# Attention into a Strassen-style MLP on one core: a new start-up order, other buffer counts, a new order at the end, and the sums of w_out moved from VectorE to GpSimd

## The chip, the core and the metric

The kernel runs on one core of a Trainium2 chip. The metric is the device time of one execution in microseconds (us), as the median over several executions. The profile of one execution gives a span that is 1.7 to 1.9 us shorter than its time (1.9 to 3.7 us in the three kernels below that begin with 92 short matmuls); spans are used only to say where time lies. A run that is over 1.5% above the fastest of the same kernel is called slow and set aside: medians are of the fast runs, and all profiles shown are of fast runs.

Names: PE is TensorE's matmuls, PEld its weight loads, DVE is VectorE, ACT is ScalarE, POOL is GpSimd. "L276" is line 276 of the kernel that the profile belongs to. The change shifts lines by five, so L672 before is L677 after (h in parts), L798 is L803 (products with w_out), L708 is L713 (h with whole 128x128 matmuls), L497 is L502 (scores), L509 is L514 (products with v), L619 is L624 (the multiplication of the silu).

## The reference

```python
# q, k, v: (8, 12, 448, 64)
scores = 1/sqrt(64) * (q @ k.T) - log(448)
attn   = 1 / (1 + exp(-scores))           # a sigmoid, no softmax
x      = (attn @ v) -> (3584, 768)
h      = x @ w_in                          # w_in  (768, 2048)
g      = h * sigmoid(h)
out    = g @ w_out                         # w_out (2048, 768), float32 out
```

## The kernel before

The kernel is a planner in Python. It keeps a model of each engine's time, decides from it in which order the instructions are emitted, and the result is one fixed stream for each engine. Twenty-four visits (four heads of one batch each) give scores, sigmoids and products with v; a piece of h takes all visits of its batch; fourteen row groups multiply g by w_out with seven products instead of eight. The seven products need sums of blocks of w_out, made once, and sums of blocks of g, made for each row group:

```python
    def tt(key, dur, deps, o, a, b_, op, prio=0):
        pl.op("DVE", dur, key, deps, lambda: nc.vector.tensor_tensor(o, a, b_, op), prio=prio)

    def sums_wo(f0, f1):                      # called for (0, 4) and (4, 8): eight sums of 128x1536
        ...
        tt(kk + (0,), d, dep, t1, a12, a11, sub, 5)
        tt(kk + (1,), d, [kk + (0,)], t2, a22, t1, sub, 5)
        tt(kk + (2,), d, [kk + (1,)], a12, a22, a12, sub, 5)
        tt(kk + (3,), d, [kk + (2,)], t4, a21, t2, sub, 5)
    ...
        def sums(self):                       # in each of 14 row groups: four sums of 128x1024
            ...
            tt(kk + (1,), 600, self.deps + old(0), s1, a21, a22, add, -1)
            tt(kk + (2,), 600, [kk + (1,)] + old(1), s2, s1, a11, sub, -1)
            tt(kk + (3,), 600, [kk + (2,), kk + (1,)], a21, a11, a21, sub, -1)
            tt(kk + (4,), 600, [kk + (2,)] + old(2), s4, a12, s2, sub, -1)
```

Both kinds of sum read two tiles in SBUF and write one there. That is the fact that this study turns on. The sums of g stand on VectorE in front of the silu multiplications, which empty the PSUM banks that TensorE needs for its next pieces of h.

Two other parts are used in the experiments. The buffer counts are `NTR = 4; NX = 4; NA = 10; NV = 6` (transposed k and q, loaded k and q, score tiles, v). And at the very start TensorE multiplies zeros to warm up, in 28 matmuls of 64x64 by 512 columns, before the first loads arrive:

```python
    def zeros(i, m):
        ...
                    nc.tensor.matmul(
                        pt[h][64 * j : 64 * j + 64, :], zero[64 * h : 64 * h + 64, :D], zero[64 * h : 64 * h + 64, :],
                        start=True, stop=True, skip_group_check=True,
                    )
```

## Time and profile before

| | before |
|---|---|
| time, median of 3 (lowest to highest) | 386.08 us (385.11 to 390.47) |
| span of the profiled execution, mean granted clock | 382.5 us, 0.996 |
| TensorE busy | 96% |
| first product with w_out starts | 86.66 us |
| one sum of g (128x1024) / of w_out (128x1536) on VectorE | 0.69 us / 0.95 us |

The prediction below shows the page's first lines, the stretches and the timelines. Two more things are needed for the comparison. First, on the page, the granted clock in 40 slices (tenths of full speed) and the chain of work that ended last, by engine and by line:

```profile
PEclk9999999999999999999999999999999999999998
...
PE 87%; DMA 7%; DVE 2%; POOL 1%; issue 1%; ACT 1%; DVEq 0%; POOLq 0%
```

The clock never falls, and TensorE carries 87% of the chain. Second, in the groups by shape, the first of the four sums of g, with its 14 executions, total busy us and mean ns; then two of these sums in VectorE's timeline, and the first product with w_out in TensorE's:

```profile
L276 DVE TENSOR_TENSOR gs<-gt 128x1024 f16<-128x1024 f16 x14 | 9.2, 688 | 0.2
...
80.04 0.68 DVE L276 TENSOR_TENSOR gs<-gt 128x1024 f16<-128x1024 f16 x1
...
81.10 0.69 DVE L276 TENSOR_TENSOR gs<-gs,gt 128x1024 f16<-128x1024 f16 x1
...
86.66 0.35 PE L798 MATMUL ps<-wo,gt 64*64 64x384 f16 x2
```

### The profile page before, as it was taken

The numbers are of one execution on the slowest core, as the hardware profiler recorded it, in microseconds if no ns is written. First come the engines' busy times: TensorE is split into PE (matmuls) and PEld (weight loads), VectorE is DVE, ScalarE is ACT, GpSimd is POOL, SyncE is SP. The second block draws the span as 40 slices with busy tenths as digits, with TensorE's granted clock in tenths as the row PEclk, the third lists the DMA queues.
The fourth block names the chain that finished last, engine by engine and source line by source line (L and its number), as shares of the span: only waits on it lengthen the run. The fifth ranks groups of instructions, "written<-read, shape, count | busy, mean of one in ns | idle before, by whom it ended". The sixth has DMA issues, their size and how long they took to land.

```text
span 382.5 us, 18036 instructions
## 1 busy us (share of the span) xinstructions
PE 367.3 (96%) x8028; PEld 305.3 (80%) x8028; DVE 203.6 (53%) x378; ACT 233.6 (61%) x506; POOL 65.0 (17%) x97
## 2 busy tenths in 40 slices
PE   6797998999999999999999999999999999999995
PEld 3565866787888989878998989878888898989763
DVE  3634988683454535454654556454645456455632
ACT  3975787677758866757637787686656863243110
POOL 9655413231220220220210220000000000000000
PEclk9999999999999999999999999999999999999998
DMA  7999999999999976993779998725132002400333
GB/s 102 196 209 205 208 209 203 157 160 152 176 194 207 135 112 130 180 189 71 96 115 181 154 143 116 124 49 79 43 71 60 3 2 47 105 22 5 74 90 90
DMA packets 80638, 46.52 MB, mean 122 GB/s; under 512 B 50609, under 2 KB 79793, under 8 KB 80561
## 3 DMA queue, kind: packets, MB, share of 16 engines
q0 software_dynamic: 25008, 22.81, 39.5%
q1 hardware_dynamic: 55552, 22.56, 35.8%
q8 instruction: 63, 1.03, 1.1%
q14 instruction: 15, 0.11, 0.1%
HBM read 45.61 MB, written 11.01 MB: 148 GB/s over the span
## 4 chain that ended last, share of the span: by engine, by line
PE 87%; DMA 7%; DVE 2%; POOL 1%; issue 1%; ACT 1%; DVEq 0%; POOLq 0%
PE ps L798 34%; PE ps L672 30%; PE ps L708 8%; PE ps L497 8%; PE ps L509 7%; DMA wi<-in_moe_w_in_dram 5%; DMA v<-in_v_dram 2%; DVE so L276 1%; PE ps L455 1%; POOL xk L219 1%; POOL xq L228 1%; DVE gt L619 0%; ACT at L947 0%; DVE xt L969 0%; DVE qT L469 0%
## 5 line engine op out<-in xcount | busy, mean ns | idle before, releaser
L672 PE MATMUL ps<-xt,wi 64*64 64x448 f16 x2304 | 164.1, 349 | 0.0
L540 ACT ACTIVATE at<-ps 128x448 f16<-128x448 f32 x252 | 121.9, 549 | 42.8 <-PE ps L497 38.7
L672 PEld LDWEIGHTS <-wi 64*64 64x64 f16 x2304 | 110.3, 107 | 14.5 <-issue 0.3
L619 DVE TENSOR_TENSOR gt<-ps,sg 128x448 f16<-128x448 f32 (+2 forms) x128 | 78.4, 622 | 78.9 <-ACT sg L614 78.6
L798 PE MATMUL ps<-wo,gt 64*64 64x384 f16 x1344 | 108.5, 323 | 0.0
L798 PEld LDWEIGHTS <-gt 64*64 64x64 f16 x1792 | 95.6, 107 | 11.7 <-issue 2.3
L614 ACT ACTIVATE sg<-ps 128x448 f16<-128x448 f32 (+2 forms) x128 | 70.2, 552 | 46.2 <-PE ps L672 31.2
L798 PE MATMUL ps<-so,gs 64*64 64x384 f16 x896 | 86.2, 323 | 0.2 <-issue 0.2
L798 PEld LDWEIGHTS <-gs 64*64 64x64 f16 x1344 | 76.2, 107 | 9.4 <-issue 1.1
L497 PE MATMUL ps<-qT,kT 64*64 64x448 f16 (+2 forms) x840 | 75.8, 316 | 2.1 <-DVE qT L469 0.8
L812 DVE SCALAR_TENSOR_TENSOR us<-ps,us 128x384 f32<-128x384 f32 x70 | 38.8, 555 | 48.7 <-PE ps L798 40.1
L947 ACT ACTIVATE at<-ps 128x512 f16<-128x512 f32 (+3 forms) x96 | 40.1, 520 | 15.6 <-PE ps L497 15.3
L708 PE MATMUL ps<-xt,wi 128*128 128x256 f16 (+1 forms) x384 | 43.3, 260 | 4.1 <-DMA wi<-in_moe_w_in_dram 2.7
L798 PE MATMUL ps<-so,gt 64*64 64x384 f16 x448 | 44.9, 323 | 0.5 <-issue 0.5
L798 PE MATMUL ps<-wo,gs 64*64 64x384 f16 x448 | 45.1, 323 | 0.0
L497 PEld LDWEIGHTS <-kT 64*64 64x64 f16 x840 | 33.8, 106 | 12.1 <-issue 7.5
L708 PEld LDWEIGHTS <-wi 128*128 128x128 f16 x384 | 32.3, 98 | 10.8 <-issue 6.7
L239 POOL DMA_DIRECT2D v<-in_v_dram x24 | 17.4, 724 | 138.7 <-PE ps L509 47.9
L509 PE MATMUL ps<-at,v 64*64 64x448 f16 (+2 forms) x840 | 40.2, 313 | 0.0
L819 ACT ACTIVATE us<-ps 128x384 f32<-128x384 f32 x28 | 14.0, 499 | 33.3 <-PE ps L798 32.7
L509 PEld LDWEIGHTS <-v 64*64 64x64 f16 x840 | 29.6, 107 | 5.2 <-issue 1.9
L552 DVE TENSOR_SCALAR xt<-ps 128x448 f16<-128x448 f32 x36 | 20.8, 620 | 21.0 <-PE ps L509 20.8
(33 smaller groups left out, 148.4 us busy)
## 6 DMA issues: line engine op xcount, KB each, us to landing
out_dram<-us SPq DMA_DIRECT2D x112, 96.0 KB, 2.7
xk<-in_k_dram POOLq DMA_DIRECT2D x24, 224.0 KB, 6.9
v<-in_v_dram POOLq DMA_DIRECT2D x24, 224.0 KB, 6.2
xq<-in_q_dram POOLq DMA_DIRECT2D x21, 224.0 KB, 8.5
wo<-in_moe_w_out_dram POOLq DMA_DIRECT2D x4, 768.0 KB, 15.4
wi<-in_moe_w_in_dram POOLq DMA_DIRECT2D x8, 192.0 KB, 7.2
wi<-in_moe_w_in_dram POOLq DMA_DIRECT2D x4, 384.0 KB, 9.7
qT<-xq SPq DMA_TRANSPOSE x32, 4.5
```

What stands on the lines that cost most here:

```text
L239: lambda: nc.gpsimd.dma_start(v16[n % NV], src(v, b, g)),
L497: nc.tensor.matmul(pt[r][64 * h : 64 * h + 64, lo : lo + (c1 - c0) * D], kT[n % NTR][64 * r : 64 * r + 64, i, 64 * h : 64 * h + 64], qT[n ...
L509: nc.tensor.matmul(pt[h][64 * j : 64 * j + 64, :N], v16[n % NV][64 * h : 64 * h + 64, j, c * D : (c + 1) * D], at[64 * h : 64 * h + 64, sl ...
L540: lambda r=r: nc.scalar.activation(at[:, sl, r], pt[r][:, :S], AF.Sigmoid, bias=NEG_LOG_S, scale=QKSCALE),
L552: lambda h=h: nc.vector.tensor_scalar_mul(x[:, 2 * g + h, :], pt[h][:, :S], SX), prio=-2,
L614: lambda: nc.scalar.activation(t[:, :ncol], src_, AF.Sigmoid, scale=ISX), prio=0,
L619: lambda: nc.vector.tensor_tensor(o, src_.rearrange("p (a t) -> p a t", a=nb), t[:, :ncol].rearrange("p (a t) -> p a t", a=nb), ALU.mult),
L672: nc.tensor.matmul(bank[64 * j : 64 * j + 64, z * N : z * N + N], wi[64 * h : 64 * h + 64, cc, f0 + 64 * j : f0 + 64 * j + 64], x[64 * h : ...
L708: nc.tensor.matmul(bank[:, z * N : z * N + N], wi[:, cc, fc * P : (fc + 1) * P], x[:, cc, self.c0 : self.c1], start=(cc == 0 and z == 0), ...
L798: nc.tensor.matmul(bank[64 * j : 64 * j + 64, :HE], lhs[64 * h : 64 * h + 64, c, 64 * j : 64 * j + 64], rhs[64 * h : 64 * h + 64, c, :], s ...
L812: lambda: nc.vector.scalar_tensor_tensor(o, bank[:, :HE], ISX, u, ALU.mult, ALU.add), prio=-2,
L947: lambda r=r, src_=src_: nc.scalar.activation(at[:, base : base + m, r, :N], src_, AF.Sigmoid, bias=NEG_LOG_S, scale=QKSCALE),
```

## The change

The intent: let readiness decide the order of the start-up instead of a fixed list; take 7.6 us of sums away from VectorE, which is busy there, and give them to GpSimd, which only issues loads; move buffers from v, k and q to score tiles; and interleave the last two row groups so that TensorE's matmuls keep overlapping. The core of the diff (the planner's loop for the middle is cut; it looks nine products ahead instead of six):

```diff
-    NTR = 4
-    NX = 4
-    NA = 10
-    NV = 6
+    NTR = 3
+    NX = 3
+    NA = 12
+    NV = 3
...
+    def tt_pool(key, n, deps, o, a, b_, op, prio=0):
+        pl.op("POOL", 100 + 2.2 * n, key, deps, lambda: nc.gpsimd.tensor_tensor(o, a, b_, op), prio=prio)
...
-        tt(kk + (0,), d, dep, t1, a12, a11, sub, 5)
-        tt(kk + (1,), d, [kk + (0,)], t2, a22, t1, sub, 5)
-        tt(kk + (2,), d, [kk + (1,)], a12, a22, a12, sub, 5)
-        tt(kk + (3,), d, [kk + (2,)], t4, a21, t2, sub, 5)
+        for z, (o, x_, y_) in enumerate(((t1, a12, a11), (t2, a22, t1), (a12, a22, a12), (t4, a21, t2))):
+            dz = dep if z == 0 else [kk + (z - 1,)]
+            if z in (0,1,2,3):
+                tt_pool(kk + (z,), (f1 - f0) * HE, dz, o, x_, y_, sub, 5)
...
-                if z and 1:
+                if z and 0:
                     between()
...
-    for b, part, full in starts:
-        it = G1(b, *((0, CA * D) if part == 0 else (CA * D, S) if part == 1 else (0, S)), 2 if part < 2 else 1, part > 0, full)
-        tasks_until(("V", b * NQ + NQ - 1, min(part, 1)))
-        it.run()
+    def start_up():
+        qs = {"S": deque(), "V": deque(), "t": deque(), "g": deque()}
...
+            for kind in ("V","S","t","g"):
...
+                if ok:
+                    return kind
...
+            if us_[-1] == NP - 1 and 1:
+                R = [w for w in R if w[1] < NP - 2]
+                R += [("p", NP - 2 + u, n) for u, n in ((0,1),(0,6),(1,1),(1,6),(0,2),(0,7),(0,5),(1,7),(1,5),(1,2),(0,4),(0,3),(1,4),(1,3))]
```

More of the change, by code (lines that the diff above doesn't have):

```diff
@@ L114, in wait, with is_ready @@
         self.flush()
-    def is_ready(self, keys):
-        return all(self.ev(k).done and self.ev(k).t <= self.t for k in keys)
+    def is_ready(self, keys, slack=0.0):
+        return all(self.ev(k).done and self.ev(k).t <= self.t + slack for k in keys)
     def pe(self, dur, key, deps, fn, lat=200.0, mode=2):
@@ L285, in sums_wo @@
         kk = ("swo", f0)
-        tt(kk + (0,), d, dep, t1, a12, a11, sub, 5)
-        tt(kk + (1,), d, [kk + (0,)], t2, a22, t1, sub, 5)
-        tt(kk + (2,), d, [kk + (1,)], a12, a22, a12, sub, 5)
-        tt(kk + (3,), d, [kk + (2,)], t4, a21, t2, sub, 5)
+        for z, (o, x_, y_) in enumerate(((t1, a12, a11), (t2, a22, t1), (a12, a22, a12), (t4, a21, t2))):
+            dz = dep if z == 0 else [kk + (z - 1,)]
+            if z in (0,1,2,3):
+                tt_pool(kk + (z,), (f1 - f0) * HE, dz, o, x_, y_, sub, 5)
+            else:
+                tt(kk + (z,), d, dz, o, x_, y_, sub, 5)
     wo_ranges = [(0, 4), (4, 8)]
@@ L602, in between @@
             if visit():
-                pace[0] = max(pace[0] + pace[1], pl.main + 600.0)
+                pace[0] = max(pace[0] + pace[1], pl.main + 300.0)
     hn = [0]
@@ L782, in old @@
                 q = 3 * pi + z - 5
-                return [("P", q // 3, use[q % 3])] if q >= 0 else []
+                return [("P", q // 3, use[q % 3])] + [("sgm", q // 3, w_) for w_ in [(2,), (4,), ()][q % 3]] if q >= 0 else []
             tt(kk + (1,), 600, self.deps + old(0), s1, a21, a22, add, -1)
@@ L1014, in task_deps @@
         if w[0] == "S":
-            return [("trk", w[1]), ("trq", w[1], 0) if w[2] == 0 and w[1] < NQ else ("trq", w[1])]
+            m = 1 if w[3] == NCH - 1 else 2
+            sd = sum([slot_deps((slot_next[0] + z) % NA) for z in range(m)], [])
+            return [("trk", w[1]), ("trq", w[1], 0) if w[2] == 0 and w[1] < NQ else ("trq", w[1])] + sd
         if w[0] == "V":
@@ L1028, in task_deps, with old_of @@
         return [("q", w[1], None)]
+    def old_of(w):
+        return [("S", w[1] - NTR, NCH - 1)] if w[0] in ("tk", "tq", "tpk", "tpq") and w[1] >= NTR else []
     def task(force=False):
@@ L1039, in task, with do_task @@
         todo.pop(0)
+        do_task(w)
+        return 1
+    def do_task(w):
         if w[0] == "S":
@@ L1055, in task @@
             transpose_pe(w[1], 2 + w[2], k_=False)
-        return 1
     def tasks_until(w, warm=True):
@@ L1063, in some_tasks @@
         n = 0
-        while n < 2 and task():
+        while n < 3 and task():
             n += 1
@@ L1075, with pick @@
         u.sums()
-    for b, part, full in starts:
-        it = G1(b, *((0, CA * D) if part == 0 else (CA * D, S) if part == 1 else (0, S)), 2 if part < 2 else 1, part > 0, full)
-        tasks_until(("V", b * NQ + NQ - 1, min(part, 1)))
-        it.run()
+    def start_up():
+        qs = {"S": deque(), "V": deque(), "t": deque(), "g": deque()}
+        for w in todo:
+            qs[w[0] if w[0] in ("S", "V") else "t"].append(w)
+        todo.clear()
+        pace[0] = 1e12
+        for b, part, full in starts:
+            it = G1(b, *((0, CA * D) if part == 0 else (CA * D, S) if part == 1 else (0, S)), 2 if part < 2 else 1, part > 0, full)
+            qs["g"] += [it] * it.n
+        under = deque()
+        def pick(slack):
+            while under and pl.is_ready([under[0]]):
+                under.popleft()
+            for kind in ("V","S","t","g"):
+                if not qs[kind]:
+                    continue
+                w = qs[kind][0]
+                if kind == "g":
+                    ok = pl.is_ready(w.deps(w.at), slack) and bank_ready()
+                else:
+                    ok = pl.is_ready(task_deps(w) + old_of(w), slack) and pair_ready()
+                    if kind == "S" and len(under) >= 3:
+                        ok = False
+                if ok:
+                    return kind
+            return None
+        while qs["g"]:
+            pl.flush()
+            kind = pick(0.0) or pick(300.0)
+            if kind is None:
+                t0 = pl.t
+                while kind is None:
+                    pl.t = max(pl.t, pl.heap[0][0])
+                    pl.flush()
+                    kind = pick(300.0)
+                m = int((pl.t - t0 - 100.0) / 214.0)
+                free = [i for i in banks if not bank_open[i] and all(pl.ev(x_).done and pl.ev(x_).t < t0 for x_ in bank_last[i])]
+                if m > 0 and len(free) > 1:
+                    i = (free[-1], free[-2])
+                    zs[0] += 1
+                    zeros(i, m)
+                    pl.fulfil(pl.ev(("zero", zs[0])), pl.t + 200.0)
+                    look(i, zs[0])
+            w = qs[kind].popleft()
+            if kind == "g":
+                w.piece()
+            else:
+                do_task(w)
+                if kind == "S":
+                    under.append(("sig", w[1], w[2], w[3]))
+        todo.extend(qs["t"])
@@ L1081 @@
+    start_up()
     blocks = [('p', [0, 1]), ('g', 2), ('p', [2, 3]), ('g', 3), ('p', [4, 5]), ('g', 4), ('p', [6]), ('g', 5), ('p', [7, 8]), ('g', 6), ('p', [9, 10]), ('g', 7), ('p', [11, 12, 13])]
@@ L1106, in cost, with due @@
         return NCC * (S / 2.4 + 2.5) if w[0] == "g" else HFC * (HE / 2.4 + 2.5)
-    def due(w):
+    def due(w, slack=0.0):
         if w[0] == "g":
             it = g1[w[1]]
-            return pl.is_ready(it.deps(it.at)) and bank_ready()
+            return pl.is_ready(it.deps(it.at), slack) and bank_ready()
         u = g2[w[1]]
@@ L1117, in due @@
             return False
-        return pl.is_ready(u.deps_of(w[2])) and (not u.new_bank(w[2]) or bank_ready())
+        return pl.is_ready(u.deps_of(w[2]), slack) and (not u.new_bank(w[2]) or bank_ready())
     def set_pace():
@@ L1135 @@
     set_pace()
+    kind_ = "p"
     while L:
-        z = 0
-        if not due(L[0]):
-            seen = set()
-            for y, w in enumerate(L[: 6]):
-                k_ = w[:2]
-                if k_ in seen:
-                    continue
-                if due(w):
-                    z = y
-                    break
-                seen.add(k_)
-            else:
-                if visit():
-                    continue
+        pl.flush()
+        near = L[: 9]
+        z = None
+        if 0:
+            z = next((y for y, w in enumerate(near[: 0]) if w[0] == kind_ and due(w, 0.0)), None)
+        if z is None:
+            z = next((y for y, w in enumerate(near) if due(w)), None)
+        if z is None:
+            z = next((y for y, w in enumerate(near) if due(w, 300.0)), None)
+        if z is None:
+            if visit():
+                continue
+            if lower_ready():
+                drain_one()
+                continue
+            if pl.heap or fifo:
+                t = [pl.heap[0][0]] if pl.heap else []
+                t += [fifo[0][0].left + 450.0] if fifo and fifo[0][0].left is not None else []
+                pl.t = max(pl.t, min(t))
+                if not (near[0][0] == "g" and g1[near[0][1]].at == 0):
+                    continue
+            z = 0
         w = L.pop(z)
+        kind_ = w[0]
         if w[0] == "g":
```

## The prediction

> **What bounds the kernel now.** I read the page first (busy shares, the 40 slices), then the table of stretches in ten-microsecond steps, then the timelines of TensorE, ScalarE, VectorE and GpSimd from 0 to 92 us and from 355 us to the end.
>
> ```profile
> span 382.5 us, 18036 instructions
> PE 367.3 (96%) x8028; PEld 305.3 (80%) x8028; DVE 203.6 (53%) x378; ACT 233.6 (61%) x506; POOL 65.0 (17%) x97
> ```
>
> TensorE is the bound, but its 96% overstates it: matmuls overlap, so a busy TensorE can be half empty. I therefore count columns. Four 64x64 matmuls share the array, one 128x128 matmul fills it. In an undisturbed run 24 full matmuls of 256 columns took 2.56 us from their start to the next row's (37.84 to 40.40), 106.7 ns each, so 0.417 ns a column; a 64x64 one then costs a quarter, 40.0 ns for 384 columns and 46.7 ns for 448. With the counts of the groups (2304 and 3136 matmuls of h and of the output, 840 + 840 of attention, 384 full ones, 448 transposes) the useful work is 334.5 us. The other 48 us are what a schedule can win, and only part of it. Before the first product with w_out (86.66 us) the same count gives 55.4 us of work: 31 us are lost in the start-up. From there to 366.41 it is about 270 us in 279.7, most of the difference being small switches of 2 to 3%: the middle is full. After 366.41 there are 228 matmuls, 9.1 us, in 11.8 us, and then 4.2 us of eviction and store.
>
> The start-up in the table of stretches (columns: stretch, then busy us and count for PE, PEld, DVE, ACT, POOL, clock, DMA share, GB/s):
>
> ```profile
> 0.00:10.00 10.00, 6.80 (x164) 3.20 (x164) 4.10 (x20) 3.52 (x7) 9.23 (x18) 1.00 0.81 107
> 10.00:20.00 10.00, 7.63 (x245) 6.04 (x244) 6.03 (x19) 9.12 (x22) 6.35 (x11) 1.00 1.31 196
> 30.00:40.00 10.00, 8.01 (x171) 6.33 (x164) 5.46 (x12) 4.45 (x11) 5.39 (x8) 1.00 1.25 202
> 50.00:60.00 10.00, 8.67 (x196) 5.94 (x194) 9.04 (x17) 7.87 (x19) 2.86 (x4) 1.00 1.20 207
> ```
>
> DMA is at its ceiling near 205 GB/s up to 70 us, so w_in's last quarter-ranges cannot come sooner. ScalarE is the second resource: its sigmoids of one batch's scores are 21.2 us (half of 18.8 + 15.8 + 4.2 + 3.5 in the groups by shape) and of its h 9 us. The timeline of TensorE shows two stalls that matter:
>
> ```profile
> 30.73 0.27 PE L708 MATMUL ps<-xt,wi 128*128 128x256 f16 x1 [0.26 <-DMA wi<-in_moe_w_in_dram]
> 32.73 0.71 PE L708 MATMUL ps<-xt,wi 128*128 128x256 f16 x5 [1.73 <-DMA wi<-in_moe_w_in_dram]
> ...
> 55.14 1.44 PE L497 MATMUL ps<-qT,kT 64*64 64x256 f16 x21
> 56.91 0.36 PE L497 MATMUL ps<-qT,kT 64*64 64x192 f16 x7 [0.34 <-DVE xt L969]
> 57.25 1.41 PE L509 MATMUL ps<-at,v 64*64 64x256 f16 x28
> 58.59 0.61 PE L708 MATMUL ps<-xt,wi 128*128 128x256 f16 x4
> 60.18 0.60 PE L708 MATMUL ps<-xt,wi 128*128 128x256 f16 x2 [0.98 <-DVE xt L969]
> ```
>
> The first is the arrival of w_in at 32.7 us. The second lies where VectorE makes the sums of w_out between the evictions TensorE waits for:
>
> ```profile
> 57.10 0.95 DVE L276 TENSOR_TENSOR wo<-wo 128x1536 f16<-128x1536 f16 x1
> 57.97 0.95 DVE L276 TENSOR_TENSOR so<-wo,so 128x1536 f16<-128x1536 f16 x1
> 58.84 0.95 DVE L276 TENSOR_TENSOR so<-wo 128x1536 f16<-128x1536 f16 x1
> 59.71 0.75 DVE L969 TENSOR_SCALAR xt<-ps 128x256 f16<-128x256 f32 x2
> ```
>
> And the end, where runs of eight stand alone instead of in pairs with the other half of the array:
>
> ```profile
> 372.13 0.81 PE L798 MATMUL ps<-wo,gt 64*64 64x384 f16 x8
> 372.78 0.81 PE L798 MATMUL ps<-so,gs 64*64 64x384 f16 x8
> ```
>
> **What the Trainium skill says.** "Trainium Kernel Development and Optimization", Performance Expectations, calls matmul busy time a bad metric because matmuls are pipelined; the trace agrees (96% busy, 334.5 us of columns in 382.5). "GPSIMD Engine Reference", section 3.1, measures a tensor_tensor add of 2048 fp32 elements at 4497 ns, about 2.2 ns an element. No GpSimd tensor_tensor is in this trace; from that page I estimate 3.4 us for 1536 elements, against 0.954 us measured on VectorE here. "SBUF — State Buffer", Who interferes with whom, says that a VectorE instruction with two SBUF inputs contends with a GpSimd instruction that reads SBUF. Nothing of it can be seen in the kernel before, where GpSimd only issues loads.
>
> **The change part by part.**
>
> *Up to the arrival of w_in.* The loads stand in the same order and DMA is at its ceiling, so this point cannot move forward. In the old stream the first scores stand before the transpose of the second k, in the new one behind it. That k landed at about 8.4 us (the transpose starts at 8.49 after a wait for it), so the first scores move from 7.41 to about 8.8 us and the first sigmoid from 7.97 to 9.35. In the new stream the last product with v of batch 0 stands before the fifth piece of h, behind ScalarE's whole 21.2 us of scores plus four silu sigmoids (2.6 us): 9.35 + 23.8 + about 0.5 of gaps gives 33.6 us; that product and filler put the fifth piece near 34.7, 2.0 us later than the 32.73 before. This is a small loss, partly paid back because that product and its scores are already done.
>
> *From there to the first product with w_out.* I priced both streams with unstalled blocks of the old timeline: 28 transposes 0.33 us; v-products 0.87 (256 columns) and 0.60 (192); scores 0.029 and 0.024 us a matmul plus 0.1 a block; h 0.1067 or 0.0833 us a matmul plus 0.1 a block for the change of tiling. The old stream prices at 50.0 us from 32.73, so it should have ended at 82.7; it ended at 86.66: 3.9 us of stalls, the ones shown plus one at 53 to 56 us. The new stream prices at 46.8 us (h is no longer cut in halves: 19 blocks for 27; no scores of batch 2 stand in it, 0.95 us that only move later). It would end at 34.7 + 46.8 = 81.5. ScalarE has some 31 us of work before the last v-product of batch 1, which then has 13.5 us of TensorE work behind it: 33.7 + 31 + 3 of gaps + 13.5 = 81, as tight as TensorE. Two resources so level never mesh fully, so I choose 1.5 us of stalls: 83.0. Against 86.66 - 0.95 = 85.7 the gain is 2.7 us.
>
> *Sums of w_out.* Eight of 0.954 us, 7.6 us, leave VectorE; their delay of TensorE is within the 3.9 us already counted. On GpSimd they take 8 x 3.4 = 27 us (estimate), and its queue is in order: the last four sums stand behind the load of the ninth v (counting from 1), which with three v buffers for six waits for batch 1's last v-product, at about 83.0 - 13.5 = 69.5. Three issues of 0.71 us and four sums give 85.2. The first product that needs them stands some 2.2 us behind the first w_out product: 85.2 too. No slack. Meanwhile VectorE has three of batch 1's two-input sums there (0.69 us each in the groups), with evictions behind them. If each waits for a GpSimd sum, up to 3 x 3.4 us of VectorE go; eight PSUM banks absorb part. I charge 1.0 us on average.
>
> *Fewer buffers (k, q 4 to 3; v 6 to 3), more for scores (10 to 12).* A load is wanted some two visits of 13 us ahead and lands in 6 to 9 us: no cost.
>
> *Middle.* Choosing among nine products instead of six can win little where little is lost: 0.3 us.
>
> *End.* The new order interleaves the last two row groups. In its stream the runs pair up to the last 8 and 16 matmuls. From 372.13 to 375.10 the old one did 40 matmuls, 1.6 us, in 2.97; I take back that 1.4 us and 0.3 of the next stretch: 1.7 us. Final eviction (0.56) and store stay.
>
> Sum: -2.7 + 1.0 - 0.3 - 1.7 = -3.7 us, from 386.08 to 382.4. The new order was doubtless chosen because something ran better with it, and my 1.5 us of stalls and 1.0 us of contention are guesses on the cautious side, so I put the point at 381.8.
>
> **Rivals.** (1) *GpSimd becomes the wait*: the sums last longer than 3.4 us or lock VectorE out. For it: no slack above. Against: banks, and products that need no sums. It gives back 3 to 6 us: 384 to 388. (2) *All stalls go*: no ScalarE coupling, no contention, 81.5 for the first product, or less if w_in still decides at 32.7. Then -4.2 to -6.2 at the start and -2 at the end: 377.5 to 380. For it: VectorE is much freer at 50 to 62 us; against: ScalarE's 60 us for two batches cannot start before 9 us. (3) *Loads late* in batch 2 from the halved v buffers behind the GpSimd sums: the tenth and eleventh k need transposes before their scores at about 110 us, with some 5 us of slack: +1 to +3.
>
> **Range and chances.** 80% range 377.5 to 387. Over 2% faster means below 378.4, which asks for nearly all of rival 2: 0.15. Over 2% slower needs rival 1 and more: 0.05. Within: 0.80.
>
> **What would show it.** First sigmoid near 9.3 us; h's fifth piece near 34.7; first w_out product near 83 (81.5 if rival 2, 86 or more if it failed); GpSimd tensor_tensors near 3.4 us, ending near 85; VectorE's 128x1024 sums at 0.69 us, or longer or waiting at 75 to 85 us under rival 1; TensorE's wait for GpSimd at the first product with so; the last 586 w_out matmuls about 1.7 us shorter. I am wrong if the first w_out product does not move by at least 1 us more than the scores postponed behind it, or if the middle, 87 to 366 us, changes by over 2 us.

## The result

The changed kernel took 401.71 us (median of 4, 399.90 to 404.05), against 386.40 us (385.11 to 390.47, 4 runs) for the kernel before. The ratio is 1.0381, with a 95% interval of 1.0287 to 1.0475. Ratios here and below are the mean time of one kernel's fast runs over that of the other's of the same rounds, so they are not quite the ratio of the medians. The kernel became slower by 15 us; the prediction of 381.8 us, and its range up to 387, were wrong.

The page after, the lines that answer to those of before:

```profile
span 400.2 us, 17994 instructions
...
PE 375.7 (94%) x8024; PEld 315.7 (79%) x8024; DVE 211.1 (53%) x368; ACT 232.8 (58%) x506; POOL 90.1 (23%) x105
...
PEclk9999968997999999998999999999999999999998
...
PE 82%; DMA 6%; DVE 5%; ACT 3%; issue 2%; POOL 0%; ACTq 0%; DVEq 0%; POOLq 0%
```

GpSimd's busy time grew by 25.1 us for eight sums. VectorE, which lost eight sums (7.6 us), is not less busy but more: 211.1 us for 203.6. The clock has fallen in the sixth, seventh and tenth slices (50 to 70 and 90 to 100 us) and a little at 180. VectorE and "issue" have grown in the chain. So the time was lost early, and VectorE has a part in it. The table of stretches (columns: stretch, its length, then busy us and count for PE, PEld, DVE, ACT, POOL, clock, DMA share, GB/s):

```profile
30.00:40.00 10.00, 9.36 (x192) 6.75 (x193) 6.37 (x16) 4.24 (x10) 6.31 (x9) 1.00 1.26 203
50.00:60.00 10.00, 6.20 (x99) 5.32 (x100) 10.00 (x10) 2.98 (x8) 6.26 (x2) 0.67 0.96 169
90.00:100.00 10.00, 5.56 (x48) 3.24 (x49) 7.95 (x11) 5.12 (x11) 2.47 (x1) 0.72 0.01 2
170.00:180.00 10.00, 6.94 (x153) 5.93 (x145) 1.82 (x4) 4.68 (x10) 0.00 (x0) 0.98 0.71 151
```

Up to 40 us the new order gains nothing yet: it makes 192 matmuls from 30 to 40 us where the old one made 171, but 32 of the 192 multiply zeros to fill a wait (the old stretch has none), and at equal work it is 0.9 us behind at 40 us. From 50 to 60 us VectorE is busy for the whole 10 us with only 10 instructions (before: 9.04 us with 17), and TensorE makes 99 matmuls for 196. From 90 to 100 us TensorE makes 48. At 170 to 180 us TensorE is short of work too, and here VectorE and ScalarE are idle with it: that is something else.

The timeline of GpSimd shows the sums of w_out; the columns are start, us, engine, line, operation, tiles, shapes and count, and in brackets the idle time before it and what ended it:

```profile
45.85 3.08 POOL L279 TENSOR_TENSOR so<-wo 128x1536 f16<-128x1536 f16 x1 [4.81 <-DMA wo<-in_moe_w_out_dram]
49.68 3.09 POOL L279 TENSOR_TENSOR so<-wo,so 128x1536 f16<-128x1536 f16 x1 [0.75 <-DMA wo<-in_moe_w_out_dram]
52.72 3.54 POOL L279 TENSOR_TENSOR wo<-wo 128x1536 f16<-128x1536 f16 x1
...
80.24 6.16 POOL L279 TENSOR_TENSOR so<-wo,so 128x1536 f16<-128x1536 f16 x2
86.35 3.09 POOL L279 TENSOR_TENSOR wo<-wo 128x1536 f16<-128x1536 f16 x1
89.39 3.07 POOL L279 TENSOR_TENSOR so<-wo,so 128x1536 f16<-128x1536 f16 x1
```

And the timeline of VectorE over the same time, the sums of g:

```profile
47.92 1.57 DVE L276 TENSOR_TENSOR gs<-gt 128x1024 f16<-128x1024 f16 x1
...
49.87 3.44 DVE L276 TENSOR_TENSOR gs<-gs,gt 128x1024 f16<-128x1024 f16 x1
...
53.71 3.11 DVE L276 TENSOR_TENSOR gt<-gt 128x1024 f16<-128x1024 f16 x1
56.74 0.68 DVE L276 TENSOR_TENSOR gs<-gt,gs 128x1024 f16<-128x1024 f16 x1
...
83.72 9.30 DVE L276 TENSOR_TENSOR gs<-gt 128x1024 f16<-128x1024 f16 x1
92.95 0.54 DVE L624 TENSOR_TENSOR gt<-ps,sg 128x384 f16<-128x384 f32 x1
```

A sum of g normally takes 0.69 us. The one that starts at 47.92 ends at 49.49; GpSimd's sum beside it ended at 48.93. The next ends at 53.31, GpSimd's at 52.77; the third at 56.82, GpSimd's at 56.26. The last begins at 83.72 and ends at 93.02; the last of GpSimd's three sums in a row ended at 92.46. In all four cases VectorE ends 0.54 to 0.56 us after GpSimd: it does its own work, nearly all of it, after GpSimd is through. At 83.72 it waited through three of GpSimd's sums, past two boundaries between them. At 52.77 it did get in at the boundary, and there GpSimd's sum became the longer one, 3.54 us for 3.09.

What TensorE makes of it, in its timeline:

```profile
33.95 1.49 PE L713 MATMUL ps<-xt,wi 128*128 128x256 f16 x12
...
53.84 0.59 PE L460 MATMUL ps<-ident,xq 64*64 64x64 f16 x28 [2.33 <-DVE gt L624]
...
57.94 1.71 PE L514 MATMUL ps<-at,v 64*64 64x256 f16 x28 [1.48 <-DMA xk<-in_k_dram]
...
93.55 0.51 PE L803 MATMUL ps<-wo,gt 64*64 64x384 f16 x4 [3.35 <-DVE gt L624]
...
178.69 0.37 PE L677 MATMUL ps<-xt,wi 64*64 64x448 f16 x1 [3.06 <-issue]
...
393.15 0.81 PE L803 MATMUL ps<-so,gt 64*64 64x384 f16 x8
393.80 1.46 PE L803 MATMUL ps<-wo,gs 64*64 64x384 f16 x16
```

TensorE waits 2.33 us and 3.35 us for the silu multiplication that stands on VectorE behind a sum of g. The wait of 1.48 us is put down to a load of k, but the load is merely the latest event the profile has there; the VectorE multiplication behind the third sum ended at 57.88, and TensorE began at 57.94. ScalarE, held up because its sg tiles are not emptied, waits in the second collision for 7.81 us, the longest such wait of the run. The line at 178.69 is the other thing: 3.06 us of "issue", in which TensorE waits for nothing that the profile shows.

A short idle of TensorE has a tail. The stretches around the first collision, at half a microsecond:

```profile
52.50:53.00 0.50, 0.00 (x0) 0.00 (x0) 0.50 (x1) 0.00 (x0) 0.50 (x2) 1.00 1.13 203
53.00:53.50 0.50, 0.00 (x0) 0.00 (x0) 0.50 (x2) 0.00 (x0) 0.50 (x1) 0.89 1.15 209
53.50:54.00 0.50, 0.16 (x13) 0.16 (x16) 0.50 (x2) 0.12 (x1) 0.50 (x1) 0.50 1.18 215
```

TensorE has been idle since 51.5 us when the granted clock (the third number from the right) is halved; the trace's own record of the clock, which has only full and half, says at 53.39 us. It stays half until 63.63 us, and after the second collision from 94.35 to 101.17 us. As an estimate from these numbers, half clock took 10.24 / 2 = 5.1 us and 6.83 / 2 = 3.4 us of TensorE's time, some of it in time when it would have waited anyhow.

"TensorE: Matmul & The Clock Gate", in the section on what is actually happening, says that the clock halves after an idle window of about 3.4 us and returns after about 3.4 us of work, and that these windows run freely instead of starting when TensorE stops. The traces agree with the windows: in each of the 14, all changes of the clock lie whole multiples of 3.41 us apart, and the two low spells here are three and two windows long. But a window need not be idle: in the one that ended at 53.39 us TensorE was busy for 45%. Cut into such windows, the 14 traces have 30 falls of the clock, all after windows in which TensorE was busy for 61% or less, and no window under 56% left the clock whole; it returned after windows of 80% and more. So where an idle stretch falls in the window matters, not only its length: in half_on_gpsimd below, TensorE was idle from 52.07 to 54.54 us, and the clock fell at 55.80 us, when it was at work again.

At equal work of TensorE (columns counted as in the prediction), the changed kernel is some 12 us behind at 100 us, still 12 at 170 us, 16.8 at 190 us and 17.7 at its end. So the two collisions cost most, a stretch around 178 us costs some 5 (3.06 us of stall and, as an estimate, half of the 3.41 us at half clock from 179.68 us on), and the middle and end give nothing back.

### The profile page after: what moved, and what is told of

It is laid out like the page before. It is cut to its first block, busy times and chain, and to the rows that moved or that the text cites. A ratio compares the mean times of both kernels' runs of the same rounds, so it can differ in the third digit from the quotient of the medians.

```text
span 400.2 us, 17994 instructions
## 1 busy us (share of the span) xinstructions
PE 375.7 (94%) x8024; PEld 315.7 (79%) x8024; DVE 211.1 (53%) x368; ACT 232.8 (58%) x506; POOL 90.1 (23%) x105
## 3 DMA queue, kind: packets, MB, share of 16 engines
q8 instruction: 63, 1.03, 1.0%
## 4 chain that ended last, share of the span: by engine, by line
PE 82%; DMA 6%; DVE 5%; ACT 3%; issue 2%; POOL 0%; ACTq 0%; DVEq 0%; POOLq 0%
PE ps L803 31%; PE ps L677 29%; PE ps L502 8%; PE ps L514 8%; PE ps L713 5%; DMA xk<-in_k_dram 5%; DVE gs L276 2%; ACT at L952 2%; DVE gt L624 1%; DMA xq<-in_q_dram 1%; PE ps L985 1%; ACT sg L619 1%; PE ps L460 1%; DVE kT L474 1%; ACT at L545 0%
## 5 line engine op out<-in xcount | busy, mean ns | idle before, releaser
L677 PE MATMUL ps<-xt,wi 64*64 64x448 f16 x2304 | 166.9, 352 | 4.1 <-issue 3.7
L677 PEld LDWEIGHTS <-wi 64*64 64x64 f16 x2304 | 114.7, 108 | 17.4 <-issue 6.1
L803 PE MATMUL ps<-wo,gt 64*64 64x384 f16 x1344 | 114.9, 326 | 3.3 <-DVE gt L624 3.3
L803 PEld LDWEIGHTS <-gt 64*64 64x64 f16 x1792 | 98.9, 108 | 15.6 <-issue 5.9
L803 PEld LDWEIGHTS <-gs 64*64 64x64 f16 x1344 | 78.9, 108 | 8.8 <-issue 0.7
L803 PE MATMUL ps<-so,gs 64*64 64x384 f16 x896 | 83.0, 326 | 0.0
L502 PE MATMUL ps<-qT,kT 64*64 64x448 f16 (+2 forms) x840 | 80.4, 334 | 2.2 <-DVE gt L624 1.1
L502 PEld LDWEIGHTS <-kT 64*64 64x64 f16 x840 | 37.5, 112 | 12.7 <-issue 8.1
L514 PE MATMUL ps<-at,v 64*64 64x448 f16 (+2 forms) x840 | 42.1, 322 | 2.7 <-DMA xk<-in_k_dram 1.5
L713 PEld LDWEIGHTS <-wi 128*128 128x128 f16 x384 | 34.8, 101 | 6.6 <-issue 2.8
```

Source lines behind the costliest of these rows:

```text
L502: nc.tensor.matmul(pt[r][64 * h : 64 * h + 64, lo : lo + (c1 - c0) * D], kT[n % NTR][64 * r : 64 * r + 64, i, 64 * h : 64 * h + 64], qT[n ...
L514: nc.tensor.matmul(pt[h][64 * j : 64 * j + 64, :N], v16[n % NV][64 * h : 64 * h + 64, j, c * D : (c + 1) * D], at[64 * h : 64 * h + 64, sl ...
L677: nc.tensor.matmul(bank[64 * j : 64 * j + 64, z * N : z * N + N], wi[64 * h : 64 * h + 64, cc, f0 + 64 * j : f0 + 64 * j + 64], x[64 * h : ...
L713: nc.tensor.matmul(bank[:, z * N : z * N + N], wi[:, cc, fc * P : (fc + 1) * P], x[:, cc, self.c0 : self.c1], start=(cc == 0 and z == 0), ...
L803: nc.tensor.matmul(bank[64 * j : 64 * j + 64, :HE], lhs[64 * h : 64 * h + 64, c, 64 * j : 64 * j + 64], rhs[64 * h : 64 * h + 64, c, :], s ...
```

## The experiments

Twelve kernels ran, in three calls of four; all gave right results. The kernel before, timed in each call on the same chip, had medians of 386.41, 385.75 and 386.45 us (22 of 23, 55 of 59 and 31 of 35 runs).

| run | fast runs, median us (fast of all) | median of all | ratio to before [95%] |
|---|---|---|---|
| sums_on_vector_same_order | 387.12 (12 of 12) | 387.12 | 1.0017 [0.9990, 1.0045] |
| sums_on_vector_replanned | 387.07 (11 of 12) | 387.17 | 1.0007 [0.9979, 1.0036] |
| old_buffers | 396.38 (3 of 4) | 397.81 | 1.0254 [1.0185, 1.0322] |
| before_sums_on_gpsimd | 392.89 (4 of 4) | 392.89 | 1.0151 [1.0118, 1.0183] |
| vector_sums_old_buffers | 389.31 (6 of 6) | 389.31 | 1.0101 [1.0054, 1.0147] |
| before_new_end | 385.73 (19 of 22) | 386.06 | 1.0000 [0.9977, 1.0024] |
| shifted_instructions | 383.78 (17 of 20) | 383.92 | 0.9968 [0.9940, 0.9996] |
| before_small_buffers | 386.83 (13 of 20) | 388.64 | 1.0029 [0.9998, 1.0060] |
| half_on_gpsimd | 393.10 (4 of 4) | 393.10 | 1.0154 [1.0093, 1.0214] |
| before_shifted | 389.66 (20 of 22) | 389.86 | 1.0086 [1.0059, 1.0113] |
| shifted_by_half | 383.00 (5 of 6) | 383.09 | 0.9891 [0.9835, 0.9947] |
| replanned_shifted | 386.18 (10 of 14) | 386.56 | 0.9970 [0.9931, 1.0010] |

My theory after the result was that GpSimd's sums lock VectorE's sums out and so cost some 14 us. Rivals were the halved buffers, and the new order as such.

### sums_on_vector_same_order

Only the engine of the eight sums is changed back; the planner still believes in GpSimd, so that TensorE's order is that of the changed kernel, instruction for instruction.

```diff
-        pl.op("POOL", ..., lambda: nc.gpsimd.tensor_tensor(o, a, b_, op), prio=prio)
+        pl.op("POOL", ..., lambda: nc.vector.tensor_tensor(o, a, b_, op), prio=prio)
```

> The changed kernel with one edit: the eight w_out sums are issued to VectorE instead of GpSimd at the same places of the schedule; the order of every TensorE instruction is identical. Theory (VectorE's two-SBUF-input sums are locked out while GpSimd sums run): the 128x1024 sums return to 0.69 us each (9.3, 3.4, 3.1 and 1.6 us before the edit), no TensorE idle of 2.3 and 3.4 us near 52 and 90 us, first w_out product near 82 to 85 us, time 383 to 391 us (the 3 us stall near 175 us may or may not stay). Rival (the new order itself is slow): the first w_out product stays beyond 90 us and the time at 395 us or more.

Measured: 387.12 us, ratio 1.0017. One word moved 14.6 us. Its timeline of VectorE at the place of the first collision:

```profile
47.67 0.68 DVE L276 TENSOR_TENSOR gs<-gt 128x1024 f16<-128x1024 f16 x1
...
48.74 0.68 DVE L276 TENSOR_TENSOR gs<-gs,gt 128x1024 f16<-128x1024 f16 x1
...
49.80 0.68 DVE L276 TENSOR_TENSOR gt<-gt 128x1024 f16<-128x1024 f16 x1
```

All sums are back at 0.68 us, though the eight sums of w_out now stand on the same engine. Because the order is the same, a milestone can be compared between such kernels: the first sum of g of the third row group starts at 94.34 us here and at 108.30 us in the changed kernel. The difference, 14.0 us, is what the collisions cost by then. From there to the end of the span it is 290.8 us here and 291.9 us there: in sum the rest differs by 1.1 us, although its stalls lie in different places. That shows the theory. It also shows that the rest of the change, without the collisions, gains nothing as it stands (387.1 for 386.4). Its timeline of TensorE says where a gain may have gone:

```profile
84.06 0.35 PE L803 MATMUL ps<-wo,gt 64*64 64x384 f16 x2
...
112.66 0.50 PE L514 MATMUL ps<-at,v 64*64 64x448 f16 x1 [3.38 <-issue]
```

The first product with w_out starts 2.6 us sooner than before (84.06 for 86.66). Then, at 112.66, comes an "issue" stall of 3.38 us like that at 178.69 in the changed kernel, and others of 0.26, 1.09, 0.59 and 0.27 us at 20.31, 45.59, 166.05 and 364.33. The kernel before has three of over 0.2 us in its profile: 0.64 us at 18.26, 0.22 at 135.45 and 0.46 at 366.41.

### sums_on_vector_replanned

The planner knows that the sums are on VectorE and orders everything anew.

```diff
-            if z in (0,1,2,3):
+            if z in ():
```

> The changed kernel with the w_out sums planned and issued on VectorE, so that the order is planned anew with them there. Theory: 379 to 388 us, faster than or level with the kernel before; the first w_out product at 80 to 85 us. Rival (new order slow, or three buffers for k, q and v slow): 393 us or more.

Measured: 387.07 us, the upper end of what was expected. The first product starts at 84.24 us, but there are "issue" stalls of 1.09 us before it and of 0.55, 3.65 (at 120.02 us) and 1.75 us (at 168.26 us) behind it. The profiled execution took 389.54 us and is one of the longer ones.

### old_buffers

The changed kernel with the buffer counts of before; the sums stay on GpSimd.

```diff
-    NTR = 3; NX = 3; NA = 12; NV = 3
+    NTR = 4; NX = 4; NA = 10; NV = 6
```

> The changed kernel with the buffer counts of before (k and q 4, v 6, scores 10), the sums still on GpSimd. Theory: the sums no longer stand behind loads that wait for v buffers, so they run in one block near 48 to 75 us; they still lock VectorE's sums of the first row group, not those of the second: 388 to 399 us. Rival (the halved buffers are the whole loss): 387 us or less, with no VectorE sum over 1 us. Rival (buffers have no part in it): 400 us or more.

Measured: 396.38 us, ratio 1.0254 (three fast runs, 393.71 to 399.25). The loss stays for the most part, so the buffers are not its cause; it is 5.3 us less than in the changed kernel, with other collisions. These came in another place than expected: GpSimd's sums ran from 62.27 to 93.67 us and met the first three sums of the second row group (3.62, 3.11 and 8.61 us). The last two, with TensorE's wait, in the timelines of TensorE and of VectorE:

```profile
94.75 0.58 PE L502 MATMUL ps<-qT,kT 64*64 64x448 f16 x3 [8.65 <-DVE gt L624]
```

```profile
82.12 3.11 DVE L276 TENSOR_TENSOR gs<-gs,gt 128x1024 f16<-128x1024 f16 x1
...
85.62 8.61 DVE L276 TENSOR_TENSOR gt<-gt 128x1024 f16<-128x1024 f16 x1
```

GpSimd's two sums here run from 87.53 to 93.67 us, and VectorE's ends at 94.23, again 0.56 us later. But it is recorded as starting at 85.62, when GpSimd was issuing loads; why it did not finish before 87.53 is not settled by this trace. The sum of 3.62 us, from 78.11, is alike: the GpSimd sum beside it ended at 79.19, loads were issued until 81.31, and VectorE ended at 81.73. In other places sums of g beside load issues take 0.68 us.

### before_sums_on_gpsimd

The kernel before, with nothing but the eight sums moved to GpSimd (the planner knows it).

```diff
-        tt(kk + (0,), d, dep, t1, a12, a11, sub, 5)      # and the other three
+        tt_pool(kk + (0,), (f1 - f0) * HE, dep, t1, a12, a11, sub, 5)
```

> The kernel before with one edit: the eight w_out sums on GpSimd. Theory: costs time only where a 128x1024 sum of VectorE meets a GpSimd sum; in this plan the first group's sums come before w_out lands and the second group's near 80 us, so 384 to 394 us, every lost microsecond beside a VectorE sum longer than 0.69 us. Rival (GpSimd sums cost by delaying the loads behind them): 390 us or more with all VectorE sums at 0.69 us and TensorE waiting for loads of k, q or v.

Measured: 392.89 us, ratio 1.0151, so the move by itself costs about 6 us. In its profile one sum of g takes 3.77 us, and the first product starts at 87.51 instead of 86.66 us. The larger loss seen in that profile is of the other kind:

```profile
107.25 0.53 PE L801 MATMUL ps<-so,gs 64*64 64x384 f16 x2 [5.89 <-issue]
```

So this run doesn't say by itself how much of its 6 us is the lock. The time was as expected, but not that every lost microsecond would stand beside a long sum.

### What the "issue" stalls are

The stalls have no releaser; all other engines run out of work with TensorE. Counting TensorE's own instructions in the program as built, from its start, I found each of some 25 stalls, in all kernels, at the 192nd or 193rd instruction of a block of 256. The page's part on DMA queues has a queue named "instruction" with 63 packets and 1.03 MB, so 16.4 KB each: 64 bytes an instruction, if each packet brings 256. "Runtime: NRT & Kernel Launch", Instruction fetch mechanics, says that instructions are fetched in 16 KiB blocks of 256, and that the cost of crossing a boundary is "mostly hidden". The theory: TensorE waits for its next block of instructions. A rival: something at that point of the work (a wait, a transfer) stalls it. In kernels of one order the stall falls on the same matmul: the one behind the first 2133 in the changed kernel (0.88 us at 124.13) and in the first experiment (3.38 us at 112.66), where the time differs by 11.5 us. That fits both theories.

### vector_sums_old_buffers

I suspected that the rush of transfers with few buffers delays the fetch, and undid the buffers with the sums on VectorE.

```diff
-            if z in (0,1,2,3):
+            if z in ():
-    NTR = 3; NX = 3; NA = 12; NV = 3
+    NTR = 4; NX = 4; NA = 10; NV = 6
```

> The changed kernel with the w_out sums on VectorE and the buffer counts of before (k and q 4, v 6, scores 10), planned anew. Theory: no lock-out, and loads spread as before, so the stalls marked issue of 3 to 4 us between 110 and 180 us (seen at the same matmul counts in every order with three buffers) are rarer: 380 to 385 us, faster than before by up to 1.5%. Rival (the new order gains nothing by itself): 385 to 388 us.

Measured: 389.31 us, ratio 1.0101: a miss. The stalls did not become rarer; its profile, of an execution of 391.37 us, has four of over 0.3 us (2.56 us at 93.67, 0.62, 1.80 at 120.83 and 2.03 at 169.84).

### before_new_end

The kernel before with only the new order of the last two row groups (the two `R` lines of the diff).

> The kernel before with one edit: the new order of the last two row groups. Prediction's term: 1.7 us less (384.8 against 386.5), the last product nearly without single runs of eight. Rival (the end is bound by the last eviction and store): within 0.5 us of before.

Measured: 385.73 us, ratio 1.0000 with an interval of 0.24% each way: no gain; 1.7 us (0.44%) is excluded. In its profile TensorE takes 26.46 us from its last matmul of h to the end of the last product, for 27.25 before, so 0.8 us are gained, 0.46 of which is a fetch stall that before has there. But from that end to the end of the span it takes 4.85 us, for 4.28: the last evictions and stores now follow each other every 1.3 us instead of 1.5 to 2.3 us, and the last store lands later.

### shifted_instructions

This separates the two theories of the stalls. The order is that of the first experiment, with sums on VectorE; only the warm-up at the start is made of 92 short matmuls of zeros instead of 28 long ones. That is 64 matmuls and 64 weight loads more, 128 instructions, half a block. If the block decides, the stalls must move to other work; if the work decides, they must stay.

```diff
-            pl.pe(m * 427, ("zero", 0), hold_, lambda: zeros(i, m))
+            pl.pe(m * 427, ("zero", 0), hold_, lambda: zeros_short(i, 23))   # 4 x 23 matmuls of 96 columns
```

> The changed kernel with the sums issued on VectorE in the same order, and 64 more short filler matmuls (128 TensorE instructions, 8 KB) at the start instead of 28 long ones. Theory (the stalls marked issue are TensorE waiting for its next 16 KB of instructions): they stay at the same counts of TensorE matmuls from the start (about 860, 2133, 3267, or others a multiple of 127 or 128 away), that is 64 matmuls earlier in the work, or vanish where the fetch is in time. Rival (a wait inside the program): they stay at the same work, at counts of about 924, 2197 and 3331. Time 383 to 390 us.

Measured: 383.78 us, ratio 0.9968; the profiled run has a span of 379.2 us. The stalls moved:

```profile
111.12 0.35 PE L803 MATMUL ps<-so,gt 64*64 64x384 f16 x1 [0.53 <-issue]
```

The matmul that stalled before has 2197 before it now and does not stall. The one with 2261 before it does, 64 matmuls or half a block further on. The other stalls in the profile are of 0.27 to 0.34 us (at 47.09, 117.51, 283.15 and 361.47). So the position in the block decides where a stall can fall. How long it lasts isn't decided by that: most boundaries cost nothing.

The kept traces settle the theory more directly, for they hold the start and the landing of every packet of the "instruction" queue. Over all 14 traces TensorE has 64 "issue" stalls of over 0.2 us. All stand at the same two neighbouring places of a block, and each ends 1.24 to 1.60 us after the landing of one packet, which by its number in the queue is the one of that block. At none of the 872 boundaries did the instruction at this place start less than 1.20 us after its packet had landed. So TensorE does wait for its instructions, and the length of a stall is how late the packet comes: for the stall of 3.38 us it started at 108.93 us and took 2.21 us (0.97 is usual), for the 5.89 us of before_sums_on_gpsimd it started 3.47 us after TensorE had stopped.

### before_small_buffers

The kernel before with NTR 3, NX 3, NA 12, NV 3.

> The kernel before with the new buffer counts alone (k and q 3, v 3, scores 12). Theory: loads bunch behind the waits for v buffers, the DMA engines are crowded when TensorE fetches instructions, 387 to 392 us with one or more stalls marked issue of over 1 us after 90 us. Rival (buffers have no part): 385.5 to 387.5 us with none.

Measured: 386.83 us, ratio 1.0029 with 1 just inside its interval: in fast runs the halved buffers alone cost at most 0.6%. Seven of its 20 runs were slow (391.06 to 394.70 us), more than of any other kernel; whether the buffers bring that about is open.

### half_on_gpsimd

The first four sums of w_out on GpSimd, the last four on VectorE, in the order of the changed kernel: one collision of the two.

```diff
-   lambda: nc.gpsimd.tensor_tensor(o, a, b_, op)
+   lambda: (nc.gpsimd if key[1] == 0 else nc.vector).tensor_tensor(o, a, b_, op)
```

> The changed kernel in the same order, with the first four w_out sums left on GpSimd and the last four issued to VectorE. Theory (lock-out): the first collision, near 48 to 57 us, stays (VectorE sums of about 1.6, 3.4 and 3.1 us), the second of 9.3 us goes; the time lies between the two, 389 to 394 us, so the second collision is worth more than the first. Rival (the loss is the length of the GpSimd queue, which stands before the loads): no VectorE sum above 1 us and 387 us.

Measured: 393.10 us, ratio 1.0154. Its timeline of VectorE has the first collision and not the second:

```profile
48.36 1.79 DVE L276 TENSOR_TENSOR gs<-gt 128x1024 f16<-128x1024 f16 x1
...
50.55 3.48 DVE L276 TENSOR_TENSOR gs<-gs,gt 128x1024 f16<-128x1024 f16 x1
...
54.41 3.10 DVE L276 TENSOR_TENSOR gt<-gt 128x1024 f16<-128x1024 f16 x1
...
84.84 0.69 DVE L276 TENSOR_TENSOR gs<-gt 128x1024 f16<-128x1024 f16 x1
```

By the medians the first collision costs 393.1 - 387.1 = 6.0 us and the second 401.7 - 393.1 = 8.6 us. By the milestone (94.34, 101.53 and 108.30 us with none, one and two) it is 7.2 and 6.8 us. The two readings agree on the sum and on the order of size; which one is larger stays open, since fetch stalls differ (2.45 us at 131.27 here).

### before_shifted

The kernel before with the 92 short matmuls at its start, to see whether that filler is simply better.

> The kernel before with the 92 short filler matmuls in place of 28 long ones, as in the shifted run, and nothing else. If the shift pays by where the 16 KB blocks of instructions begin in the work: the kernel before, which had only 0.5 us of such stalls, does not gain, 385 to 387 us. If the filler itself pays: 383 to 384.5 us.

Measured: 389.66 us, ratio 1.0086 with the interval above 1: a miss, it became slower. Its timeline of TensorE shows, among stalls of 1.07, 0.55 and 0.36 us:

```profile
164.41 0.38 PE L497 MATMUL ps<-qT,kT 64*64 64x448 f16 x2 [1.65 <-issue]
```

(Its first sigmoid also began 2.1 us later than before's, 10.08 for 7.97 us, but h's piece that waits for w_in began only 0.35 us later.) So the short filler is not a gain in itself. The stalls of over 0.2 us add up to 3.6 us here, to 1.3 us in the kernel before. The filler moves the block boundaries, and that helped one order and hurt another.

### shifted_by_half

As shifted_instructions with 60 short matmuls: 32 matmuls, 64 instructions, a quarter of a block.

> The changed kernel in the same order with the sums on VectorE, and 60 short filler matmuls (32 more than 28, 64 instructions) at the start. Theory (fetch of instructions): the stalls stay 192 or 193 instructions into a block of 256; the time depends on what work stands there, 382 to 388 us, between the unshifted 387.1 and the shifted 383.9. Rival (chance of the chips): as the shifted run within 0.5 us.

Measured: 383.00 us, ratio 0.9891, interval 0.9835 to 0.9947. It is faster than both kernels, by 1.1% against before. The 0.8 us that it is below shifted_instructions lie outside the span: the fast runs of both have a median span of 381.2 us. Its first product:

```profile
82.65 0.35 PE L803 MATMUL ps<-wo,gt 64*64 64x384 f16 x2
```

### replanned_shifted

The replanned kernel with the 92 short matmuls.

> The changed kernel with the sums planned and issued on VectorE, and the 92 short filler matmuls: a candidate to beat both. If the shift works here too: 382 to 385 us, against 387.2 unshifted; stalls of 1 us and more gone. If its gain was particular to that order: 386 to 388 us.

Measured: 386.18 us, ratio 0.9970, interval across 1: no gain, as the second alternative had it. Its profile still has stalls, 1.99 us at 113.82 the longest.

## Why the prediction was wrong, point by point

**The arrival of w_in: right.** The first sigmoid began at 9.25 us (predicted 9.35), h's fifth piece at 33.95 us (34.7). That the loads were at a "ceiling" near 205 GB/s is not shown: they kept to that rate up to 50 us, but sums_on_vector_same_order moved 284 GB/s from 113 to 115 us.

**The way to the first product with w_out: right without the collisions.** Predicted was 83.0 us. With the sums on VectorE in the same order it started at 84.06 us, of which 1.09 us is a fetch stall, and at 82.65 us where that stall was absent (shifted_by_half). Both have the sums of w_out on VectorE, so the gain did not need them moved, although the prediction counted their delay of TensorE among the 3.9 us of stalls. With the collisions it started at 93.55 us.

**The sums of w_out: the step that failed.** Their durations were right: 3.07 to 3.54 us each, for an estimate of 3.4. They ended at 92.46 us instead of 85.2, because GpSimd's queue waits for work that the first collision had delayed: the ninth load of v was issued at 78.08 us, against 72.02 in the twin (sums_on_vector_same_order) and 69.5 in the prediction. The step that failed is "I charge 1.0 us on average" for VectorE's contention. It measured 14.0 us at the milestone and 14.6 us between the medians of the changed kernel and its twin with the sums on VectorE. Three things were missing in it. I counted "up to 3 x 3.4 us" for the collision at 75 to 85 us only, and did not look for sums of g near the first three sums of w_out at 46 to 56 us. I trusted that eight PSUM banks absorb part of the lock; but one locked sum holds every eviction that stands behind it on VectorE (none ran from 83.72 to 92.95 us), so TensorE and ScalarE both stopped. And a stopped TensorE loses its clock, which I had not charged. Rival 1 named the mechanism, but as 3 to 6 us.

**Fewer buffers: no cost, as predicted,** as far as could be seen. In before the halved buffers cost nothing that 13 fast runs could resolve (ratio 1.0029, interval 0.9998 to 1.0060), and in the changed kernel the old ones left it 2.5% slower than before.

**The middle, -0.3 us: wrong.** "The middle is full" was true of before's profile, but a new order puts other matmuls at the boundaries of TensorE's instruction blocks. Without the collisions, and with the prediction's other terms (-2.7, -0.3 and -1.7 us), 381.4 us would be expected from 386.08; the twin took 387.12, so 5.7 us are missing. Behind the first product with w_out its profile has 4.24 us of fetch stalls (3.38 + 0.59 + 0.27) and, as an estimate, 1.7 us lost to the half clock of 112.72 to 116.13 us, before's 0.68 (0.22 + 0.46). That accounts for 5.3 of the 5.7, if the profiled runs are typical. Where the stalls were fewer the gain appeared: 383.00 us with 1.19, 0.93 and 0.28 us of them (the 0.93 us has another releaser on the page, but ends 1.45 us after its packet's landing).

**The end, -1.7 us: not found.** The order by itself gave nothing in before (385.73 us, ratio 1.0000). The step counted only to the last product; the stores behind it took 0.6 us more. In the changed kernel the last matmul of h to the last product's end is 25.71 us for 27.25 before, and the rest of the span 4.94 us for 4.28: at most 0.9 us.

**What stays open.** Why some packets of instructions come so late that TensorE stalls for up to 5.9 us, while most come in time: stalls came with a DMA share of 1.28 (109.2 to 112.7 us of the first experiment), 1.41 (101.3 to 107.3 us of before_sums_on_gpsimd), and also of 0.43 (175.6 to 178.7 us of the changed kernel). Also open is when VectorE gets the lock at a boundary of GpSimd's instructions: it did at 52.77 us, and twice did not between 83.7 and 92.5 us. A version with the lock removed while the sums stay on GpSimd could not be made, since both kinds of sum need two inputs in SBUF.

## What to carry to other kernels

Before moving elementwise work to an idle GpSimd, look for VectorE instructions with two SBUF inputs in the same stretch, and take each as lasting until GpSimd's instruction ends, and perhaps its whole run of them, together with everything that stands behind it on VectorE. Here 7.6 us taken off VectorE cost 14 us. When two fixed orders are compared within 1 or 2%, read the stalls without a releaser first: here a shift of TensorE's 16,270 instructions by 64 or 128 moved the time by -4.1 to +3.2 us, as much as the new order was worth.

## What the Trainium skill lacked or had wrong

- "SBUF — State Buffer", SBUF: two separate sides: the shared ports are said to be held for one whole instruction. The trace shows a VectorE sum shut out over three GpSimd sums in a row, 9.30 us instead of 0.69, and in another place let in between two. The page has ratios for single instructions, but no size in a kernel: here 14.0 us for two collisions.
- "GPSIMD Engine Reference", section 3.1, has the figure for fp32 only (4497 ns for 2048 elements, 2.2 ns an element). In 16 bits with two SBUF inputs, 1536 elements took 3.09 us alone, 2.0 ns an element, and 3.54 us with VectorE in between.
- "Runtime: NRT & Kernel Launch", Instruction fetch mechanics, calls the cost of a block boundary "mostly hidden". Most boundaries were, but TensorE stalled for up to 5.89 us at one, always at instruction 192 or 193 of 256 and until 1.24 to 1.60 us after the block's packet had landed, and the four stalls in the profile of vector_sums_old_buffers add up to 7.0 us (2.56 + 0.62 + 1.80 + 2.03).
- "TensorE: Matmul & The Clock Gate", What's actually happening: the clock is said to halve after an idle window of about 3.4 us. In the changed kernel it was halved after a window in which TensorE was busy for 45%, 1.9 us after it fell idle, and over the 14 traces after windows with up to 61%. The page gives no such share.
